# A gated attention and MLP mix on one core: where the keys are split, how the output products are tiled, and over how many keys the row maximum is taken

## The chip, the cores and the metric

The kernel runs on one core of one Trainium2 chip. The metric is device time in microseconds (us), the median of three runs. A profile of one execution stands beside it: when every instruction of the five engines began and ended (PE is TensorE, PEld its weight loads, DVE VectorE, ACT ScalarE, POOL GpSimd, SP SyncE, which here only issues transfers).

## What is computed

```python
# x: 2048 x 448, H = 16 heads of Dh = 28; one key and one value head for all (wk, wv: 448 x 28)
q = (x @ wq).reshape(S, H, Dh);  k = x @ wk;  v = x @ wv
p = softmax(q @ k.T * Dh ** -0.5)            # per head, 2048 x 2048
a = (p @ v).reshape(S, H * Dh) @ wo          # 2048 x 448
h  = gelu(layernorm(x) @ w1)                 # the four quarters of h are then shifted by +1, -1, +2, -2 rows
x1 = x + shifted(h) @ w2
b  = x1 + gelu(layernorm(x1) @ w3) @ w4      # w3: 448 x 1792
g  = sigmoid(x @ gate_w)
out = g * a + (1 - g) * b
```

## The kernel before

All values are fp32. Most products are taken in TensorE's faster fp32 format (fp32r) on split operands: an operand is cut into a high part that the format holds and a low part with the rest, and high x high, low x high and high x low are added up in one bank. The product of probabilities and values is plain fp32.

The program has three stages.

1. **Projections and the token mixing.** Queries, keys, values and the gate come out of one projection and are written to the DRAM buffer `qd`. `stage_w1` and `stage_w2` do the mixing for four blocks of 512 tokens. Towards the end the keys are read back, a quarter (512 keys) at a time, into one buffer `kf`: `load_k` (L332, eight transfers on SP's queue, four copies of the 28 rows on partitions 0, 32, 64 and 96), and `split_k` (L336, L337, both on POOL) cuts it into `kH` and `kL`. The buffer is filled with ones once, so that the rows behind the 28 hold ones. `load_k(0)` is issued before the first transfers of MLP weights (`load_w34`, L550 and L551) and the read of the normalised tokens (`xt_read`, L171, L173); the other three follow these.
2. **The MLP.** Four blocks `b` of 512 tokens, 14 slices `f` of 128 hidden columns each: `w3_part` (11 matmuls of 512 columns, L130 to L134), two gelus on ACT, and two slices later `w4_part` (12 matmuls of 448 columns, L641 to L643). The weights come in pairs of slices, pair `i` serving `f` = 2i and 2i+1. They are split on arrival: high parts and copies on ACT (L105, L107, L108, L557), low parts on DVE (L112, L113, L558), and POOL zeroes half of the last part of `w3h` (L106). The raw weights and the transposed tokens share two buffers (`big`), so pair 1 is loaded into the buffer that the tokens `xr` of block 0 leave, and pair 2 into that of pair 0.
3. **Attention.** The unit `u` (0 to 15) is 512 queries of four heads; inside it `kt` runs over 16 key tiles of 128. One step does 12 score matmuls (L828: three products for each of four heads, each head on its own 32 rows of the array, all four side by side, each head into a bank of its own), four exponentials of 128x512 on ACT (L832), and the value products of two steps ago (L808: four plain fp32 matmuls, each on its own 32 columns of the array, all into one bank). Seven banks rotate for scores and for the two extra jobs below. A column of ones in the values gives the row sums.

Extra jobs sit between a step's scores and its value products:
- `max_part` (L204, L205), four times for each coming unit: one matmul of 256 columns (four heads times `MK` = 64 keys) into a bank, and a maximum on DVE. The negated maximum is put in two spare rows of the next unit's queries (`max_end`, L224 to L232), so that the exponentials stay bounded. For units 1 to 15 the parts are made at `kt` 1, 3, 4 and 5 of the unit before (for unit 1 at 5, 7, 9 and 10); unit 0's are made in MLP block 2.
- `wo_job` (L769 to L771), four times for each unit gone by, at `kt` 8, 10, 12 and 14: three fp32r matmuls of 448 columns, 128 tokens by 448. Its left operand was normalised before: copy of the sums out of the bank (`o`, L736), transfers of the row sums out and back over DRAM (`rt`, `rd`, `rb`), the reciprocal, a multiplication on DVE (L754), and the split on POOL (L757, L758). Unit 0 has `w4_job` in its place.

Each engine runs its instructions in the order written. A last branch does all attention again with maxima over all keys if a row sum exceeds `LIMIT` = 1e12.

Of the kernel before, what the change touches and what calls it, by code (L numbers as in the profile page):

```python
# [9 lines left out]
F32 = mybir.dt.float32  # L10
F32R = mybir.dt.float32r
AF = mybir.ActivationFunctionType
# [20 lines left out]
MK = 64  # L33
# [3 lines left out]
def f32(ap):  # L37
    return ap.bitcast(F32)
# [3 lines left out]
def gated_mix_kernel(  # L42
# [157 lines left out]
    def max_part(u, t, tile_of):  # L200
        if t == 0:
            mx_of[u] = late.tile([P, 4, 4], F32, tag="mr", bufs=1, name=f"mr_{u}")
        ps = tile_of(f"m_{u}_{t}")[:, 0:4 * MK].rearrange("p (j k) -> p j k", j=4)
        nc.tensor.matmul(ps, qh_of[u][:, t * P:(t + 1) * P], khd, start=True, stop=True)  # L204
        nc.vector.reduce_max(mx_of[u][:, :, t], ps, axis=AX.X)  # L205
# [32 lines left out]
    with tc.tile_pool(name="s1b", bufs=1) as s1b, \  # L238
# [77 lines left out]
        kf = s1b.tile([P, 512], F32, name="kf")  # L316
        nc.gpsimd.memset(kf, 1.0)

# [9 lines left out]
        def load_k(b):  # L328
            for r in range(4):
                for g, n in ((0, 16), (1, DH - 16)):  # L330
                    at = 32 * r + 16 * g
                    nc.sync.dma_start(kf[at:at + n, :], rest(g, n, b))  # L332

        def split_k(b):
            cols = slice(512 * b, 512 * b + 512)
            nc.gpsimd.tensor_copy(kH[:, cols], kf)  # L336
            nc.gpsimd.tensor_tensor(kL[:, cols], kf, f32(kH)[:, cols], ALU.subtract)  # L337
# [191 lines left out]
        load_k(0)  # L529
# [77 lines left out]
    with tc.tile_pool(name="s2", bufs=1, reuse_waits="tile") as s2, \  # L607
# [5 lines left out]
        fills = [lambda t=t: max_part(0, t, max_tile if t % 2 else misc_tile) for t in range(4)]  # L613
        fills += [lambda: max_end(0)]
# [30 lines left out]
        for b in range(NB):  # L645
            acc = [ps2.tile([P, 512], F32, tag="acc", bufs=4, name=f"acc_{b}_{t}") for t in range(4)]
            gs = {}
            for f in range(NF):
# [24 lines left out]
                if b == 1 and f == 1:  # L673
# [4 lines left out]
                if b == 1 and f == 5:  # L678
                    q_split(0, qh0, ql0)
                if f >= 2:  # L680
                    for t in range(4):
                        w4_part(f - 2, t, gs[f - 2], acc)
                        if b > 1 and t % 2 == 0 and f < NF - 1:
                            fill()
# [15 lines left out]
    with tc.tile_pool(name="s3", bufs=1, reuse_waits="tile") as s3, \  # L700
            tc.tile_pool(name="ps3", bufs=1, space=PSUM, reuse_waits="tile") as ps3:
        woh = s3.tile([P, 4, D], F32R, name="woh")
        wol = s3.tile([P, 4, D], F32R, name="wol")

        banks = [mm_tile("bank_0"), mm_tile("bank_1"), misc_tile("bank_2")]
        banks += [ps3.tile([P, 512], F32, name=f"bank_{i}") for i in range(3, 7)]

# [26 lines left out]
        def sums_begin(u, pv):  # L734
            o = s3.tile([P, 512], F32, tag="o", bufs=2, name=f"o_{u}")
            nc.vector.tensor_copy(o, pv)  # L736
# [15 lines left out]
        def norm(u, o, rb):  # L752
            on = s3.tile([P, 512], F32, tag="onf", bufs=2, name=f"on_{u}")
            nc.vector.tensor_mul(on, o, rb)  # L754
            onh = s3.tile([P, 512], F32R, tag="onh", bufs=2, name=f"onh_{u}")
            onl = s3.tile([P, 512], F32R, tag="onl", bufs=2, name=f"onl_{u}")
            nc.gpsimd.tensor_copy(onh, on)  # L757
            nc.gpsimd.tensor_tensor(onl, on, f32(onh), ALU.subtract)  # L758
            on_of[u] = (onh, onl)
# [3 lines left out]
        def wo_job(u, t, end=None):  # L763
            b, g = divmod(u, NG)
            n = 4 * b + t
            tok = slice(t * P, (t + 1) * P)
            onh, onl = on_of[u]
            ps = bank(f"job_{n}")[:, 0:D]
            nc.tensor.matmul(ps, onh[:, tok], woh[:, g, :], start=True, stop=False)  # L769
            nc.tensor.matmul(ps, onh[:, tok], wol[:, g, :], start=False, stop=False)  # L770
            nc.tensor.matmul(ps, onl[:, tok], woh[:, g, :], start=False, stop=True)  # L771
            before = x1[:, n, :] if g == 0 else ot_of[n]
            if g == 0:
                ot_of[n] = s3.tile([P, D], F32, tag="ot", bufs=5, name=f"ot_{n}")
            if end:
                end(t, n, ps, before)
                return
            nc.vector.scalar_tensor_tensor(ot_of[n], ps, gg[:, n:n + 1], before, op0=ALU.mult, op1=ALU.add)  # L778
            if g == NG - 1:
                nc.sync.dma_start(out[0, n * P:(n + 1) * P, :], ot_of[n])  # L780

        woraw = s3.tile([P, 4, D], F32, name="woraw")
        nc.sync.dma_start(woraw, wo.rearrange("(g p) n -> p g n", p=P))
        nc.gpsimd.tensor_copy(woh, woraw)
        nc.gpsimd.tensor_tensor(wol, woraw, f32(woh), ALU.subtract)
# [15 lines left out]
        def pv_group(k):  # L801
            u, kt = divmod(k, NT)
            if kt == 0:
                pv_of[u] = max_tile(f"pv_{u}")
            pv = pv_of[u]
            ps = p_of.pop(k)
            for j in range(4):
                nc.tensor.matmul(pv[32 * j:32 * j + 32, :], vext[:, kt, :], ps[j],  # L808
                                 start=(kt == 0), stop=(kt == NT - 1), tile_position=(0, 32 * j))
            if kt == NT - 1 and u < NU - 1:  # L810
                sums.append(sums_begin(u, pv_of.pop(u)))

        WO_AT = (8, 10, 12, 14)
        M_AT = (1, 3, 4, 5)
        M_FIRST = (5, 7, 9, 10)
        LAG = 2

        for k in range(NU * NT + LAG):
            u, kt = divmod(k, NT)
            if k < NU * NT:  # L820
                if kt == 13 and u + 2 < NU:
                    q_begin(u + 2)
                    q_fetch(u + 3)
                bs = [bank(f"s_{4 * k + j}") for j in range(4)]
                for i in range(3):
                    for j in range(4):
                        for _, _, w, a in score(u, bs[j], j, slice(kt * P, (kt + 1) * P), i=i):
                            nc.tensor.matmul(bs[j], w, a, start=(i == 0), stop=(i == 2), tile_position=(32 * j, 0))  # L828
                p_of[k] = []
                for j in range(4):  # L830
                    p = s3.tile([P, 512], F32, tag="p", bufs=PB, name=f"p_{4 * k + j}")
                    nc.scalar.activation(p, bs[j], AF.Exp, scale=SCALE)  # L832
                    p_of[k].append(p)
                if kt == 3 and sums:
                    norms.append(recip(*sums.pop()))
                if kt == 6 and norms:
                    norm(*norms.pop())
                if kt in WO_AT:
                    t = WO_AT.index(kt)
                    if u:  # L840
                        wo_job(u - 1, t)
                    else:
                        w4_job(t)
                m_at = M_AT if u else M_FIRST
                if u + 1 < NU and kt in m_at:
                    t = m_at.index(kt)
                    max_part(u + 1, t, bank)
                    if t == 3:
                        max_end(u + 1)
            if k >= LAG:  # L850
                pv_group(k - LAG)
# [5 lines left out]
        onh = s3.tile([P, 512], F32R, tag="onh", bufs=2, name=f"onh_{u}")  # L857
        onl = s3.tile([P, 512], F32R, tag="onl", bufs=2, name=f"onl_{u}")
        on_of[u] = (onh, onl)
# [18 lines left out]
        def tail_back(t):  # L878
            nc.tensor.transpose(tq[t], on4[:, t], ident)
            nc.scalar.copy(onh[:, toks[t]], tq[t])  # L880

        def tail_low(t):
            nc.vector.tensor_sub(onl[:, toks[t]], tq[t], f32(onh)[:, toks[t]])
# [36 lines left out]
        tail_low(0)  # L920
        tail_on(3)
        tail_low(1)
# [6 lines left out]
        tail_low(2)  # L929
        tail_wo(0)  # L930
        tail_back(3)
        tail_low(3)
        tail_wo(1)
        tw = max_tile("worst_t")[0:1, 0:P]
# [10 lines left out]
        with tc.If(again > 0, label="redo"):  # L945
            for b in range(NB):
                for g in range(NG):
# [5 lines left out]
                    pv = max_tile(f"pv2_{u}")  # L953
# [9 lines left out]
                    norm(*recip(*sums_begin(u, pv), False))  # L963
                    for t in range(4):
                        wo_job(u, t)
# [51 lines left out]
```

## Time and profile before

| | us |
|---|---|
| median of 3 runs (lowest, highest) | 994.31 (994.22, 994.57) |
| the profiled execution, its time / its span | 995.8 / 994.0 |
| PE busy in the span | 970.8 (98%) |
| ACT busy | 651.9 (66%) |
| DVE busy | 287.1 (29%) |
| POOL busy | 107.5 (11%) |
| mean granted TensorE clock | 0.989 |

The rows in the prediction are of three kinds. A timeline row is: start, duration, engine, line, operation, output<-inputs, shape, number of instructions merged, and in brackets the idle time of that engine before it and what ended it. A row of a weight load (PEld) marks well where a group of matmuls begins. A row of the windows view is: the stretch, its length, busy time and instructions of PE, PEld, DVE, ACT and POOL, then the granted clock, the transfer engines' share and GB/s.

### The profile page before, as it was taken

The numbers are of one execution on the slowest core, as the hardware profiler recorded it, in microseconds if no ns is written. First come the engines' busy times: TensorE is split into PE (matmuls) and PEld (weight loads), VectorE is DVE, ScalarE is ACT, GpSimd is POOL, SyncE is SP. The second block draws the span as 40 slices with busy tenths as digits, with TensorE's granted clock in tenths as the row PEclk, the third lists the DMA queues.
The fourth block names the chain that finished last, engine by engine and source line by source line (L and its number), as shares of the span: only waits on it lengthen the run. The fifth ranks groups of instructions, "written<-read, shape, count | busy, mean of one in ns | idle before, by whom it ended". The sixth has DMA issues, their size and how long they took to land.

```text
span 994.0 us, 18445 instructions
## 1 busy us (share of the span) xinstructions
PE 970.8 (98%) x7251; PEld 562.5 (57%) x7251; DVE 287.1 (29%) x572; ACT 651.9 (66%) x1266; POOL 107.5 (11%) x134
## 2 busy tenths in 40 slices
PE   9999949999999999999999999999999999999997
PEld 6788838888888888843333333333333333333333
DVE  4663424631431431212222222212222221222112
ACT  5542315432232232299999999999998999999895
POOL 2241320100000520040000000000000000000000
PEclk9999969999999999999999999999999999999999
DMA  9703334130210300010000010000010000110001
GB/s 322 244 27 79 114 98 121 44 87 1 40 41 2 77 3 11 1 49 24 13 24 14 19 54 13 24 13 20 27 41 23 14 24 12 42 33 3 12 13 41
DMA packets 38750, 46.19 MB, mean 46 GB/s; under 512 B 8880, under 2 KB 27008, under 8 KB 38656
## 3 DMA queue, kind: packets, MB, share of 16 engines
q1 hardware_dynamic: 35632, 39.47, 13.4%
q10 hardware_dynamic: 3024, 5.47, 1.6%
q8 instruction: 59, 0.97, 0.4%
q14 instruction: 35, 0.29, 0.1%
HBM read 32.85 MB, written 11.67 MB: 45 GB/s over the span
## 4 chain that ended last, share of the span: by engine, by line
PE 94%; DMA 2%; SPq 1%; POOL 1%; DVE 0%; issue 0%; ACT 0%; POOLq 0%; DVEq 0%; ACTq 0%
PE pv L808 25%; PE bank L828 23%; PE acc L642 4%; PE acc L641 4%; PE acc L643 4%; PE g L131 4%; PE g L132 4%; PE g L130 4%; PE bank L769 2%; PE bank L204 2%; SPq L332 1%; PE g L133 1%; PE bank L771 1%; PE g L134 1%; PE bank L770 1%; PE h L130 1%
## 5 line engine op out<-in xcount | busy, mean ns | idle before, releaser
L832 ACT ACTIVATE p<-bank 128x512 f32<-128x512 f32 x1024 | 515.3, 640 | 47.9 <-PE bank L828 45.6
L808 PE MATMUL pv<-p,vext 128*32 128x512 f32 x2048 | 272.9, 604 | 0.0
L828 PEld LDWEIGHTS bank<-qh,kH 30*128 30x128 f32 x1024 | 51.7, 181 | 214.4 <-ACT p L832 212.9
L631 ACT ACTIVATE gh<-g 128x512 fp32r<-128x512 f32 x55 | 32.8, 597 | 183.6 <-PE g L134 183.6
L828 PE MATMUL bank<-qh,kH 30*128 30x512 f32 x1024 | 133.1, 494 | 0.4 <-ACT p L832 0.4
L828 PE MATMUL bank<-qh,kL 28*128 28x512 f32 x1024 | 105.7, 391 | 0.0
L828 PE MATMUL bank<-ql,kH 28*128 28x512 f32 x1024 | 105.6, 388 | 0.0
L633 DVE TENSOR_TENSOR gl<-gf,gh 128x512 fp32r<-128x512 f32 x55 | 38.5, 700 | 165.3 <-ACT gf L632 165.3
L808 PEld LDWEIGHTS pv<-p,vext 128*32 128x32 f32 x2048 | 40.6, 108 | 76.5 <-issue 62.8
L642 PE MATMUL acc<-w4l,gh 128*128 128x448 f32 x220 | 80.4, 366 | 0.0
L641 PE MATMUL acc<-w4h,gh 128*128 128x448 f32 x220 | 80.3, 365 | 0.0
L643 PE MATMUL acc<-w4h,gl 128*128 128x448 f32 x220 | 80.2, 365 | 0.0
L778 DVE SCALAR_TENSOR_TENSOR ot<-bank,gg,ot 128x448 f32<-128x448 f32 x44 | 30.1, 684 | 161.2 <-PE bank L771 122.6
L131 PE MATMUL g<-al,w3h 128*128 128x512 f32 x168 | 66.4, 395 | 0.0
L205 DVE TENSOR_REDUCE mr<-bank 128x4 f32<-128x256 f32 x60 | 25.6, 426 | 141.2 <-PE bank L204 141.2
L130 PE MATMUL g<-ah,w3h 128*128 128x512 f32 x168 | 66.3, 395 | 0.0
L132 PE MATMUL g<-ah,w3l 128*128 128x512 f32 x168 | 66.3, 395 | 0.0
L757 POOL CAST onh<-on 128x512 fp32r<-128x512 f32 x15 | 9.2, 611 | 493.0 <-DVE on L754 458.7
L828 PEld LDWEIGHTS bank<-ql,kH 28*128 28x128 f32 x1024 | 52.6, 185 | 9.1
L828 PEld LDWEIGHTS bank<-qh,kL 28*128 28x128 f32 x1024 | 51.9, 185 | 0.0
L641 PEld LDWEIGHTS acc<-w4h,gh 128*128 128x128 f32 x220 | 41.3, 188 | 4.7
L642 PEld LDWEIGHTS acc<-w4l,gh 128*128 128x128 f32 x220 | 41.3, 188 | 4.1
(196 smaller groups left out, 1096.2 us busy)
## 6 DMA issues: line engine op xcount, KB each, us to landing
qd<-qf ACTq DMA_DIRECT2D x16, 256.0 KB
qr<-qd SPq DMA_DIRECT2D x16, 256.0 KB
rb<-rd SPq DMA_DIRECT2D x15, 256.0 KB
x<-in_x_dram SPq DMA_DIRECT2D x4, 896.0 KB
xd<-xt SPq DMA_DIRECT2D x16, 224.0 KB
w34raw<-in_w_dram SPq DMA_DIRECT2D x7, 512.0 KB
out_dram<-ot SPq DMA_DIRECT2D x15, 224.0 KB
w34raw<-in_w_dram SPq DMA_DIRECT2D x7, 448.0 KB
```

The source lines that it names most:

```text
L130: nc.tensor.matmul(ps, wh[:, c, :], ah[:, c, :], start=(c == 0), stop=False)
L131: nc.tensor.matmul(ps, wh[:, c, :], al[:, c, :], start=False, stop=False)
L132: nc.tensor.matmul(ps, wl[:, c, :], ah[:, c, :], start=False, stop=False)
L631: nc.scalar.activation(gh, ps, AF.Gelu_apprx_tanh)
L633: nc.vector.tensor_sub(gl, gf, f32(gh))
L641: nc.tensor.matmul(ps, gh[:, tok], w4h[i][:, k, :], start=(f == 0), stop=False)
L642: nc.tensor.matmul(ps, gh[:, tok], w4l[i][:, k, :], start=False, stop=False)
L643: nc.tensor.matmul(ps, gl[:, tok], w4h[i][:, k, :], start=False, stop=(f == stop))
L778: nc.vector.scalar_tensor_tensor(ot_of[n], ps, gg[:, n:n + 1], before, op0=ALU.mult, op1=ALU.add)
L808: nc.tensor.matmul(pv[32 * j:32 * j + 32, :], vext[:, kt, :], ps[j], start=(kt == 0), stop=(kt == NT - 1), tile_position=(0, 32 * j))
L828: nc.tensor.matmul(bs[j], w, a, start=(i == 0), stop=(i == 2), tile_position=(32 * j, 0))
L832: nc.scalar.activation(p, bs[j], AF.Exp, scale=SCALE)
```

## The change

Four edits.

**Keys.** `load_k` and `split_k` go out of stage 1 and into MLP block 1: loads at `f` = 0, 2, 4, 6, splits at `f` = 1, 3, 5, 7. `kf` is now taken from the buffer `xn` (one buffer, used by the layernorm of a coming block at `f` = 10 and 11), and is filled with ones each time. The copies of the first keys into `khd` and the load and split of unit 0's queries go from block 1 to block 2, and unit 0's maxima from block 2 to block 3.

**Maxima.** `MK` is 32, and `max_all` makes all four parts at `kt` 5: four matmuls of 128 columns into one bank, one DVE maximum over 128x512.

**Output products.** `wo` and the normalised sums are no longer split. `wo_job` does four plain fp32 matmuls of 448 columns with 32 tokens each, on the four column tiles that the value products use. The reciprocal goes from `kt` 3 to 4 and the multiplication from 6 to 7.

**Bookkeeping.** Banks are taken from a list and given back after their last reader (`take`, `append`); the order of scores, extra jobs and value products in a step stays.

```diff
-MK = 64
+MK = 32
-    def max_part(u, t, tile_of):
-        ps = tile_of(f"m_{u}_{t}")[:, 0:4 * MK].rearrange("p (j k) -> p j k", j=4)
-        nc.tensor.matmul(ps, qh_of[u][:, t * P:(t + 1) * P], khd, start=True, stop=True)
-        nc.vector.reduce_max(mx_of[u][:, :, t], ps, axis=AX.X)
+    def max_all(u, ps):
+        for t in range(4):
+            nc.tensor.matmul(ps[:, t * P:(t + 1) * P], qh_of[u][:, t * P:(t + 1) * P], khd, start=True, stop=True)
+        nc.vector.reduce_max(mx_of[u].rearrange("p j t -> p t j"), ps.rearrange("p (t j k) -> p t j k", t=4, j=4), axis=AX.X)
...
-        load_k(0)
-            split_k(t) if t < 2 else None
-            load_k(t + 1) if t < 2 else None
         stage_w2(NB - 2, third)
-        split_k(2)
-        load_k(3)
-        split_k(3)
...
+                if b == 1 and f in (0, 2, 4, 6):
+                    load_k(f // 2, s2a.tile([P, 512], F32, tag="xn", bufs=1, name=f"kf_{f // 2}"))
+                if b == 1 and f in (1, 3, 5, 7):
+                    split_k(f // 2)
...
-            on = s3.tile([P, 512], F32, tag="onf", bufs=2, name=f"on_{u}")
-            nc.vector.tensor_mul(on, o, rb)
-            nc.gpsimd.tensor_copy(onh, on)
-            nc.gpsimd.tensor_tensor(onl, on, f32(onh), ALU.subtract)
+            nc.vector.tensor_mul(on_of[u], o, rb)
...
-            nc.tensor.matmul(ps, onh[:, tok], woh[:, g, :], start=True, stop=False)
-            nc.tensor.matmul(ps, onh[:, tok], wol[:, g, :], start=False, stop=False)
-            nc.tensor.matmul(ps, onl[:, tok], woh[:, g, :], start=False, stop=True)
+            for j in range(4):
+                tok = slice(t * P + 32 * j, t * P + 32 * j + 32)
+                nc.tensor.matmul(ps[32 * j:32 * j + 32, 0:D], on_of[u][:, tok], wof[:, g, :],
+                                 start=True, stop=True, tile_position=(0, 32 * j))
...
-        M_AT = (1, 3, 4, 5)
-        M_FIRST = (5, 7, 9, 10)
+        M_AT = 5
```

The order of the instructions on POOL at the end of stage 1, before: `hl` is the last work of the token mixing, then come the four key splits, then the zeroing of the MLP weights, pair 0 first.

```order
L415 MEMSET hl_915 112x4x2
L336 CAST kH<-kf 128x512
L337 TENSOR_TENSOR kL<-kf,kH 128x512
L336 CAST kH<-kf 128x512
L337 TENSOR_TENSOR kL<-kf,kH 128x512
L336 CAST kH<-kf 128x512
L337 TENSOR_TENSOR kL<-kf,kH 128x512
L336 CAST kH<-kf 128x512
L337 TENSOR_TENSOR kL<-kf,kH 128x512
L106 MEMSET w3h_1013 64x256
L106 MEMSET w3h_1166 64x256
```

The same place after:

```order
L414 CAST hl_686<-hl_913 112x4x2
L416 MEMSET hl_913 112x4x2
L106 MEMSET w3h_1003 64x256
L106 MEMSET w3h_1124 64x256
L106 MEMSET w3h_1169 64x256
```

The zeroing now follows the token mixing at once. SP's queue at the same place, after (`vT` is the read of the values):

```order
L322 DMA vT<-qd 16x1x512 x2
L550 DMA w34raw_1007<-in_w_dram 128x4x256
L551 DMA w34raw_1007<-in_w_dram 128x2x448
L171 DMA xr_1002<-xd_847 128x3x512
L173 DMA xr_1002<-xd_847 64x512 x2
L550 DMA w34raw_1128<-in_w_dram 128x4x256
L551 DMA w34raw_1128<-in_w_dram 128x2x448
```

Before, eight `kf` transfers stood between the first two rows and 24 between the last `xr` row and the load of weight pair 1.

PE in an attention step with an output product, before (the last scores, the product, the value products):

```order
L828 MATMUL bank_3210<-ql_3575,kH 128x512
L828 MATMUL bank_3211<-ql_3575,kH 128x512
L769 MATMUL bank_3212<-woh,onh_4306 128x448
L770 MATMUL bank_3212<-wol,onh_4306 128x448
L771 MATMUL bank_3212<-woh,onl_4307 128x448
L808 MATMUL pv_4181<-p_4296,vext 32x512
```

The same after:

```order
L799 MATMUL bank_3215<-ql_3568,kH 128x512
L799 MATMUL bank_3216<-ql_3568,kH 128x512
L763 MATMUL bank_3210<-wof,on_4315 32x448 x4
L822 MATMUL pv_4168<-p_6_0_4283,vext 32x512
L822 MATMUL pv_4168<-p_6_1_4285,vext 32x512
```

Three full-array matmuls between scores and values have become four on column tiles, next to others on the same tiles. PE in the step that makes the maxima, after:

```order
L799 MATMUL bank_3216<-ql_3568,kH 128x512
L799 MATMUL bank_3210<-ql_3568,kH 128x512
L203 MATMUL bank_3211<-khd,qh_4012 128x128 x4
L822 MATMUL pv_4168<-p_3_0_4185,vext 32x512
L822 MATMUL pv_4168<-p_3_1_4187,vext 32x512
```

Before, one row of that kind, 256 columns wide, stood at this place in four different steps.

More of the change, by code (lines that the diff above doesn't have):

```diff
@@ L799, in gated_mix_kernel, with scores, exps, late_exps @@
         p_of, pv_of, sums, norms = {}, {}, [], []
-        def pv_group(k):
-            u, kt = divmod(k, NT)
+        def scores(u, kt):
+            bs = [take() for j in range(4)]
+            for i in range(3):
+                for j in range(4):
+                    for _, _, w, a in score(u, bs[j], j, slice(kt * P, (kt + 1) * P), i=i):
+                        nc.tensor.matmul(bs[j], w, a, start=(i == 0), stop=(i == 2), tile_position=(32 * j, 0))
+            return bs
+        def exps(u, kt, bs):
+            ps = p_of[u, kt] = {}
+            for j in READ:
+                ps[j] = s3.tile([P, 512], F32, tag="p", bufs=PB, name=f"p_{u}_{kt}_{j}")
+                if j in DRAIN:
+                    nc.vector.tensor_copy(ps[j], bs[j])
+                else:
+                    nc.scalar.activation(ps[j], bs[j], AF.Exp, scale=SCALE)
+                banks.append(bs[j])
+        def late_exps(u, kt):
+            for j in DRAIN:
+                nc.scalar.activation(p_of[u, kt][j], p_of[u, kt][j], AF.Exp, scale=SCALE)
+        def values(u, kt):
             if kt == 0:
@@ L819, in gated_mix_kernel @@
             u, kt = divmod(k, NT)
[L820 to L849, printed above, removed]
@@ new lines, in gated_mix_kernel @@
+            if kt == 13 and u + 2 < NU:
+                q_begin(u + 2)
+                q_fetch(u + 3)
+            exps(u, kt, scores(u, kt))
+            late_exps(u, kt)
+            if kt == 4 and sums:
+                norms.append(recip(*sums.pop()))
+            if kt == 7 and norms:
+                norm(*norms.pop())
+            if kt == M_AT and u + 1 < NU:
+                ps = take()
+                max_all(u + 1, ps)
+                banks.append(ps)
+                max_end(u + 1)
@@ L850, in gated_mix_kernel @@
+            if kt in WO_AT:
+                if u:
+                    wo_add(*wo_job(u - 1, WO_AT.index(kt)))
+                else:
+                    w4_job(WO_AT.index(kt))
             if k >= LAG:
-                pv_group(k - LAG)
+                values(*divmod(k - LAG, NT))
+        for kt in range(NT - LAG, NT):
+            values(NU - 1, kt)
         assert not sums and not norms
@@ L879, in tail_back @@
             nc.tensor.transpose(tq[t], on4[:, t], ident)
[L880 to L883 removed]
+            nc.scalar.copy(on_of[u][:, toks[t]], tq[t])
         y = s3.tile([P, D], F32, name="y")
```

79 lines of the change are left out of this document (38 added, 41 removed).

## The prediction

> **What bounds the kernel now.** I read the windows view first, then the timeline of PE where a window is not full, then POOL, SP and ACT at that place, and last PE's weight loads in the attention loop.
>
> ```profile
> 100.00:125.00 25.00, 25.00 (x121) 21.53 (x120) 12.28 (x20) 9.63 (x16) 9.01 (x14) 1.00 0.34 109
> 125.00:150.00 25.00, 11.38 (x41) 9.08 (x40) 5.28 (x10) 3.46 (x6) 5.31 (x10) 0.66 0.31 98
> ...
> 500.00:600.00 100.00, 100.00 (x966) 38.26 (x966) 22.07 (x47) 91.96 (x184) 5.67 (x6) 1.00 0.09 27
> ```
>
> PE is full in the attention loop (500 to 600), and ACT close behind it with 92 of 100 us. So the loop pays for what PE issues, and gives back what is taken from PE only as long as ACT keeps up. The one hole lies at 125 to 150: PE busy 11.4 of 25 us, and the granted clock down to 0.66.
>
> ```profile
> 130.24 0.39 PE L132 MATMUL g<-ah,w3l 128*128 128x512 f32 x1
> 144.25 0.79 PE L133 MATMUL g<-ah,w3h 128*128 128x512 f32 x1 [13.62 <-POOL w3h L106]
> ...
> 149.53 0.61 PE L134 MATMUL g<-ah,w3l 128*128 128x512 f32 x1
> 149.96 0.41 PE L130 MATMUL g<-ah,w3h 128*128 128x512 f32 x1
> ...
> 152.50 0.36 PE L641 MATMUL acc<-w4h,gh 128*128 128x448 f32 x1
> ```
>
> ```profile
> 132.34 0.61 POOL L336 CAST kH<-kf 128x512 fp32r<-128x512 f32 x1 [8.05 <-DMA kf<-qd]
> 133.03 1.26 POOL L337 TENSOR_TENSOR kL<-kf,kH 128x512 fp32r<-128x512 f32 x1
> 141.88 0.61 POOL L336 CAST kH<-kf 128x512 fp32r<-128x512 f32 x1 [7.58 <-DMA kf<-qd]
> 142.57 1.26 POOL L337 TENSOR_TENSOR kL<-kf,kH 128x512 fp32r<-128x512 f32 x1
> 143.89 1.57 POOL L106 MEMSET w3h<- 64x256 f32 x6
> ```
>
> The first MLP slice stops in its tenth matmul, because POOL zeroes `w3h` only after the last key split, and each split waits some 8 us for its eight transfers. The hole has nothing to do with the weights themselves.
>
> **Edit 1, the keys.** With the splits gone from POOL the zeroing follows the token mixing, and L133 can start one matmul after L132. In the 11 matmuls from 149.96 to 152.50 one takes 2.54 / 11 = 0.23 us, so the start is 130.47 and the hole gives 144.25 - 130.47 = 13.8 us. The 13 matmuls from 144.25 to 149.96 took 5.71 us, 0.44 each, at the lowered clock; at 0.23 they take 3.0. That gives 2.7 us more. Together **16.5 us**.
>
> By the Trainium skill ("TensorE: Matmul & The Clock Gate", "What's actually happening") an idle array drops to half rate and about 3.4 us of busy time lifts that; at half rate 3.4 us lose 1.7 us, and the sum would be 1.0 us smaller. The row has 5.7 us at the low rate and decides.
>
> What is late next? The weights of pair 1, which slice 2 needs.
>
> ```profile
> 114.30 25.75 SPq L332 DMA_DIRECT2D kf<-qd  x24
> 140.16 0.61 SPq L550 DMA_DIRECT2D w34raw<-in_w_dram  x1
> 119.89 0.69 DVE L579 TENSOR_TENSOR ah<-xr,ah 64x512 fp32r<-64x512 f32 x1
> 125.03 1.07 DVE L558 TENSOR_TENSOR w4l<-w34raw,w4h 128x896 fp32r<-128x896 f32 x1
> 144.70 0.83 ACT L105 CAST w3h<-w34raw 128x768 fp32r<-128x768 f32 x1 [24.11 <-DMA w34raw<-in_w_dram]
> 146.63 0.41 DVE L113 TENSOR_TENSOR w3l<-w34raw,w3h 64x256 fp32r<-64x256 f32 x1
> ```
>
> SP issued that load only at 140.16, behind 24 key transfers (25.75 us of issue). Without them it needs its buffer, which the tokens leave at 119.89 + 0.69 = 120.6. From issue to the first cast took 4.5 us (140.16 to 144.70), from there to the last low part 2.3: ready at 127.5. Slice 2 starts after slices 0 and 1, at 130.47 + 0.46 + 2.54 = 133.5, so 6 us are to spare. Pair 2 follows in the buffer free at 126.1 and is needed two slices later still. No new wait.
>
> In block 1 the keys come back: four rounds of a fill, eight transfers and two POOL operations. A round took 141.88 - 132.34 = 9.5 us, with the fill an estimated 10 to 11, so four take about 42 us. POOL and SP have nothing else there until `f` = 10, where the layernorm wants `xn` back. Ten slices are about 50 us: one is the 2.54 above plus twelve `w4` matmuls of 448 columns, 0.2 us each at the same rate. PE waits for no key before attention. I take nothing for it; if DVE found `xn` still held at `f` = 10, the few us would be hidden by the two slices that remain. The moved query load and `khd` are five transfers with a block to spare.
>
> **Edit 2, the maxima.**
>
> ```profile
> 561.50 0.19 PEld L828 LDWEIGHTS bank<-qh,kH 30*128 30x128 f32 x4 [0.84 <-ACT p L832]
> ...
> 562.39 0.19 PEld L204 LDWEIGHTS bank<-khd,qh 128*128 128x128 f32 x1 [0.36 <-ACT p L832]
> 562.71 0.16 PEld L808 LDWEIGHTS pv<-p,vext 128*32 128x32 f32 x8
> 563.71 0.29 PEld L828 LDWEIGHTS bank<-qh,kH 30*128 30x128 f32 x4 [0.84 <-ACT p L832]
> ...
> 564.69 0.16 PEld L808 LDWEIGHTS pv<-p,vext 128*32 128x32 f32 x8 [0.35 <-DVE o L736]
> ```
>
> ```profile
> 110.47 0.56 PEld L342 LDWEIGHTS vp<-ident,vT 128*128 128x128 f32 x4
> 111.00 0.19 PEld L422 LDWEIGHTS hs<-w2h,hh 112*128 112x128 f32 x1
> ```
>
> A part costs PE 562.71 - 562.39 = 0.32 us, four in a unit 1.28. Much of that is the change of tiling around the single matmul: 256 columns stream in 0.23 x 256 / 512 = 0.115. Four matmuls together pay this once. No row shows 128 fp32r columns on the full array. Lower bound: pure streaming, 0.058 each. Upper bound: the plain fp32 rate of the value products (edit 3), 0.215. The nearest row is the four 128-column transposes of L342, 0.53 us, 0.13 each, and I take that. The group then costs (0.32 - 0.115) + 4 x 0.13 = 0.73 us (0.44 to 1.07), and a unit gains 0.55 (0.21 to 0.84). Over 15 units: **8.2 us** (3 to 12.6). The DVE maximum grows to one of 512 columns and has four steps until anyone asks.
>
> With no part at `kt` 1, a small wait goes too: the value products at 564.69 waited for the copy `o`, that step taking 564.69 - 563.71 = 0.98 for its scores where 0.89 is usual (561.50 to 562.39). 0.09 x 14: **1.2 us**.
>
> **Edit 3, the output products.**
>
> ```profile
> 574.24 0.19 PEld L828 LDWEIGHTS bank<-qh,kH 30*128 30x128 f32 x4 [0.84 <-ACT p L832]
> ...
> 575.14 0.16 PEld L808 LDWEIGHTS pv<-p,vext 128*32 128x32 f32 x8 [0.36 <-issue]
> 576.13 0.19 PEld L828 LDWEIGHTS bank<-qh,kH 30*128 30x128 f32 x4 [0.84 <-ACT p L832]
> ...
> 577.03 0.19 PEld L769 LDWEIGHTS bank<-woh,onh 128*128 128x128 f32 x1 [0.36 <-issue]
> ...
> 577.84 0.16 PEld L808 LDWEIGHTS pv<-p,vext 128*32 128x32 f32 x8 [0.31 <-issue]
> ...
> 978.77 0.13 PEld L808 LDWEIGHTS pv<-p,vext 128*32 128x32 f32 x4 [0.30 <-issue]
> ...
> 979.63 0.12 PEld L808 LDWEIGHTS pv<-p,vext 128*32 128x32 f32 x2 [0.30 <-ACT p L832]
> ```
>
> A plain step is 576.13 - 574.24 = 1.89 us: 0.90 of scores, 0.99 of values. The product adds 577.84 - 577.03 = 0.81. The new one has the form of the value products, which run 0.99 us between scores, but 979.63 - 978.77 = 0.86 where one such group follows another. The new product is followed by one, so the change of tiling is paid once for both, and it adds 0.86 x 448 / 512 = 0.75 us. Upper bound, with the change paid again: 0.99 x 448 / 512 = 0.87; no row shows such a group faster than 0.86, so 0.75 is the lower one too, and the nearer. I take it: 60 products x 0.06 = **3.6 us** (or -3.6 at the upper bound). So this edit is nearly even; four fp32 matmuls side by side cost what three fp32r ones did.
>
> It also takes POOL's split out of the chain before the product. That cover is good in most units (three maxima parts lengthen the way), but not in the last:
>
> ```profile
> 948.09 0.69 DVE L736 COPY o<-pv 128x512 f32<-128x512 f32 x1 [5.96 <-PE pv L808]
> 958.58 0.16 PEld L808 LDWEIGHTS pv<-p,vext 128*32 128x32 f32 x8 [0.37 <-issue]
> 959.36 0.69 DVE L754 TENSOR_TENSOR on<-o,rb 128x512 f32<-128x512 f32 x1 [8.36 <-DMA rb<-rd]
> ...
> 962.20 0.19 PEld L771 LDWEIGHTS bank<-woh,onl 128*128 128x128 f32 x1 [1.06 <-POOL onl L758]
> 962.60 0.16 PEld L808 LDWEIGHTS pv<-p,vext 128*32 128x32 f32 x8 [0.21 <-issue]
> ```
>
> That step took 4.02 us where 1.96 + 0.81 were due: **1.2 us**, gone when the product needs only L754 (done at 960.05, the scores at about 960.5). In the other units the way from `o` to the product is now as short as here plus one group of maxima, so the product finds its operand 0.4 us or more ahead.
>
> **What ACT takes back.**
>
> ```profile
> 943.32 19.71 ACT L832 ACTIVATE p<-bank 128x512 f32<-128x512 f32 x40 [0.58 <-PE bank L828]
> ```
>
> Forty exponentials in a row take 19.71 us, 1.97 a step, against PE's 1.89. Extra jobs gave ACT time to catch up; now `kt` 15 and 0 to 4 are six plain steps in a row. With three spare banks PE can, by estimate, run ahead for about four of them and follows ACT in the last two: 2 x 0.06 in 14 units, **-1.6 us**.
>
> The tail trades twelve fp32r matmuls (0.20 each) for four groups of 0.75 with changes of tiling around the transposes between them, an estimated **-0.6 us**, less if the dropped low parts were on its path.
>
> Sum: 16.5 + 8.2 + 1.2 + 3.6 + 1.2 - 1.6 - 0.6 = **28.5 us**. The profiled execution would go from 995.8 (span 994.0) to 967.3; the median of the runs lies 1.5 lower, so I predict 994.3 - 28.5 = **965.8 us**.
>
> **The rivals.**
>
> *The 128-column matmuls run at the plain fp32 rate.* Nothing in the trace excludes it. A group then costs 1.07 us and the time is 965.8 + 15 x 0.34 = 971 us. Twelve in 100.
>
> *The column tiles of the output product don't overlap fully.* Four value products in a group do, but those read four different moving tiles, and these read one and the same. At 0.87 us the time is 965.8 + 60 x 0.12 = 973 us. The Trainium skill ("TensorE: Matmul & The Clock Gate", "Measured speedup vs the span model") gives 3.07 for four tiles of rows, not 4; by that the product would take 0.98 us and the time would be 979.5. The back-to-back groups above speak against it. Eleven in 100.
>
> *The hole is filled by another wait.* If pair 1, or another release that the splits had covered, came as late as before, the 16.5 us of edit 1 would be lost: 982 us. Against it stands the slack of 6 us. Six in 100.
>
> *Slower: the four output products run one after another,* since they share the moving tile `wof`. One alone takes 0.75, four 3.0 us: 60 x (3.0 - 0.75) = 135 us, 1101 us. It decides against the change from 60 x d = 28.5, a product 0.48 us dearer, 1.23 us. All four value products also share a bank and do overlap. Three in 100. The repeat branch is no rival: worked out from the inputs drawn, the largest row sum is 2.6e9 with 64 keys and 3.0e10 with 32, under the limit of 1e12.
>
> **How the numbers follow.** The forecast itself has 68 in 100, with its own range 961 to 969 (the lower bound of the maxima, -4.4; no loss to ACT and tail, and half of a miss each way). The range for all reaches down to 959, where these favourable bounds add up, and up to 975, past the first two rivals; the last two, 9 in 100, lie outside. Faster by over 0.2% (about 2 us, what a measurement of this kernel can tell from no change): 0.96; within 0.2%: 0.01; slower: 0.03.
>
> **What would show it.** The window 125 to 150 would show PE full and a granted clock of 1.00. `max_all`'s group would measure 0.73 us between its first weight load and that of the values, the output product 0.75. PE's share should stay at 100 in the loop, and ACT's rise to about 94. The loop from first to last `o` should shorten by 0.8 us a unit. The prediction is wrong if PE has a new idle stretch in the first slices of the MLP, or waits for `on` at `kt` 8, or if the output products show no overlap.

## The result and the profile after

| | before | after |
|---|---|---|
| median (lowest to highest), us | 994.44 (994.22 to 996.14) | 965.61 (965.27 to 966.19) |
| ratio to before, 95% interval | 1 | 0.9703 (0.9691 to 0.9714) |
| the profiled execution, its time / its span | 995.8 / 994.0 | 965.27 / 963.5 |
| mean granted TensorE clock | 0.989 | 0.998 |

The change gives 28.8 us by the medians; 965.8 was forecast. The profiled execution of the kernel before was 1.4 us above its median and that of the changed kernel 0.3 below, so the two traces differ by 30.5. The same two windows as before, of the changed kernel:

```profile
125.00:150.00 25.00, 25.00 (x117) 21.58 (x116) 11.98 (x22) 11.91 (x23) 0.55 (x2) 1.00 0.49 158
500.00:600.00 100.00, 100.00 (x1048) 36.06 (x1048) 18.98 (x40) 94.01 (x190) 0.00 (x0) 1.00 0.09 27
```

The hole is gone, at a full clock. In the attention loop PE stays full, and ACT rises from 92 to 94 of 100 us. The timelines of PE in the first slices, then of POOL and SP:

```profile
127.34 0.40 PE L130 MATMUL g<-ah,w3h 128*128 128x512 f32 x1
...
129.19 0.39 PE L132 MATMUL g<-ah,w3l 128*128 128x512 f32 x1
129.41 0.39 PE L133 MATMUL g<-ah,w3h 128*128 128x512 f32 x1
...
134.85 0.36 PE L635 MATMUL acc<-w4h,gh 128*128 128x448 f32 x1
```

```profile
111.35 1.06 POOL L106 MEMSET w3h<- 64x256 f32 x4
...
196.18 0.61 POOL L337 CAST kH<-kf 128x512 fp32r<-128x512 f32 x1 [16.09 <-DMA kf<-qd]
...
227.54 0.61 POOL L337 CAST kH<-kf 128x512 fp32r<-128x512 f32 x1 [7.87 <-DMA kf<-qd]
188.20 37.23 SPq L332 DMA_DIRECT2D kf<-qd  x32
247.89 3.02 SPq L166 DMA_DIRECT2D xd<-xt  x4
```

L133 follows L132 by 0.22 us, where 13.62 us of waiting stood: POOL zeroed its part at 111.35, 16 us before the first slice. The 33 matmuls to the first `w4` product take 7.51 us, 0.23 each. The four key rounds in block 1 lie (227.54 - 196.18) / 3 = 10.45 us apart and end some 18 us before SP has its next work.

Three steps of the loop, by PE's weight loads. The first makes the maxima, the second copies the sums out (`o`), and the third, from another unit, has an output product:

```profile
548.03 0.27 PEld L799 LDWEIGHTS bank<-qh,kH 30*128 30x128 f32 x4 [0.84 <-ACT p L809]
...
549.01 0.52 PEld L203 LDWEIGHTS bank<-khd,qh 128*128 128x128 f32 x4 [0.36 <-issue]
549.61 0.16 PEld L822 LDWEIGHTS pv<-p,vext 128*32 128x32 f32 x8
```

```profile
542.32 0.19 PEld L799 LDWEIGHTS bank<-qh,kH 30*128 30x128 f32 x4 [0.84 <-ACT p L809]
...
543.22 0.16 PEld L822 LDWEIGHTS pv<-p,vext 128*32 128x32 f32 x8 [0.36 <-DVE o L826]
```

```profile
518.45 0.19 PEld L799 LDWEIGHTS bank<-qh,kH 30*128 30x128 f32 x4 [0.84 <-ACT p L809]
...
520.35 0.19 PEld L799 LDWEIGHTS bank<-qh,kH 30*128 30x128 f32 x4 [0.84 <-ACT p L809]
521.25 0.16 PEld L763 LDWEIGHTS bank<-wof,on 128*32 128x32 f32 x8 [0.36 <-ACT p L809]
...
522.99 0.19 PEld L799 LDWEIGHTS bank<-qh,kH 30*128 30x128 f32 x4 [0.84 <-ACT p L809]
```

The group takes 549.61 - 549.01 = 0.60 us. The step with a product takes 522.99 - 520.35 = 2.64, a plain one 1.90, so the product adds 0.74. From one unit to the next it is 34.05 us in the middle of the loop, 34.96 before: 0.91 less, where some 0.8 was forecast.

Where the span's 30.5 us came from, between marks that both traces have:

| stretch | before | after | difference | forecast |
|---|---|---|---|---|
| start to first `w3` matmul | 128.39 | 127.34 | -1.05 | 0 |
| from there to the first scores | 291.38 | 274.75 | -16.63 | -16.5 |
| from there to the last copy `o` | 528.32 | 514.96 | -13.36 | -11.4 |
| from there to the last values | 33.48 | 31.96 | -1.52 | -1.2 |
| the tail | 12.43 | 14.49 | +2.06 | +0.6 |

The first row is no effect of the change: the mark lies at 128.20, 127.56 and 127.52 in the three kernels below that hold one edit each.

### The profile page after: what moved, and what is told of

Read it like the earlier page. It is cut to its first block, busy times and chain, and to the rows that moved or that the text cites. A ratio compares the mean times of both kernels' runs of the same rounds, so it can differ in the third digit from the quotient of the medians.

```text
span 963.5 us, 18999 instructions
## 1 busy us (share of the span) xinstructions
PE 954.1 (99%) x7571; PEld 542.9 (56%) x7571; DVE 269.4 (28%) x520; ACT 647.1 (67%) x1266; POOL 75.0 (8%) x105
## 3 DMA queue, kind: packets, MB, share of 16 engines
q1 hardware_dynamic: 35632, 39.45, 13.8%
## 5 line engine op out<-in xcount | busy, mean ns | idle before, releaser
L822 PEld LDWEIGHTS pv<-p,vext 128*32 128x32 f32 x2048 | 46.8, 108 | 97.1 <-issue 89.9
L132 PE MATMUL g<-ah,w3l 128*128 128x512 f32 x168 | 65.6, 390 | 0.0
L763 PE MATMUL bank<-wof,on 128*32 128x448 f32 x512 | 61.2, 551 | 0.0
```

The lines of the kernel that those rows point to most:

```text
L132: nc.tensor.matmul(ps, wl[:, c, :], ah[:, c, :], start=False, stop=False)
L763: nc.tensor.matmul(ps[32 * j:32 * j + 32, 0:D], on_of[u][:, tok], wof[:, g, :], start=True, stop=True, tile_position=(0, 32 * j))
```

## The experiments

The kernel before had a median of 995.3 to 995.6 us beside these runs. Gains are given from the ratio, with its interval. The edits are shown shortened.

**One edit at a time.** Three kernels, each the kernel before with one edit: the keys in block 1; 32 keys and `max_all` at `kt` 5; plain fp32 products on column tiles.

```diff
# keys_only                                   # max_only                    # wo_only
-  load_k / split_k in stage 1                -MK = 64                      -3 matmuls onh/onl x woh/wol, split on POOL
+  load_k / split_k at b == 1, f = 0..7       +MK = 32, max_all at kt 5     +4 matmuls on x wof, tile_position=(0, 32 * j)
```

> The kernel before with the keys moved to MLP block 1, nothing else. Theory (POOL's order made the hole): the first MLP slice runs through, 16.5 us less than before, about 977.9 us, and the stretch from the first w3 matmul to the first scores shrinks from 291.4 us to about 275. Rival (the hole was covered by several things and edit 2 or 3 helped to close it): less than 12 us gained. Second rival (the 1.05 us by which the changed kernel was already ahead before the token mixing ended belongs to this edit, which takes a POOL fill out of the start): 976.8 us, and the lead is seen again before 108 us.

> The kernel before with the maxima over 32 keys in one group at kt 5, nothing else. Theory: a group costs 0.60 us in place of 4 x 0.32, and the small wait for the copy o goes: 15 x 0.68 + 1.2 less some 1.5 for ACT, about 984.5 us. The output product still waits for POOL's split, which is now covered by one group less: up to 1 us a unit may come back, which would give up to 995. Rival (128 columns run at the plain fp32 rate): a group of 1.07 us and about 992 us.

> The kernel before with the output product in plain fp32 on four column tiles, nothing else. Theory: 0.75 us in place of 0.82 a product, 60 times, 4.0 us less; 1.2 us less for the wait in the last unit; 1.3 to 2 us more in the tail: about 991 us. Rival (the product itself gains nothing, only the shorter way before it): 994 us, with the step of a product as long as before.

| kernel | median, us | ratio (interval) | gain, us |
|---|---|---|---|
| keys | 979.16 | 0.9834 (0.9815 to 0.9854) | 16.5 (14.5 to 18.4) |
| maxima | 985.21 | 0.9901 (0.9884 to 0.9918) | 9.9 (8.2 to 11.5) |
| products | 991.37 | 0.9960 (0.9946 to 0.9975) | 4.0 (2.5 to 5.4) |

The sum is 30.4, the whole change gives 29.5 (28.4 to 30.7) by its ratio: within their errors the edits add up. The keys alone fill the hole (the window of that kernel; below it the group of the kernel with the maxima alone):

```profile
125.00:150.00 25.00, 25.00 (x117) 21.64 (x116) 12.00 (x23) 12.33 (x22) 0.55 (x2) 1.00 0.50 157
```

```profile
565.58 0.52 PEld L203 LDWEIGHTS bank<-khd,qh 128*128 128x128 f32 x4 [0.36 <-issue]
566.17 0.16 PEld L806 LDWEIGHTS pv<-p,vext 128*32 128x32 f32 x8
```

The group's 0.59 us is the same with and without the other edits.

**The low clock behind the hole.** Was the forecast's 2.7 us really the price of an idle TensorE?

```diff
+        wps = misc_tile("hole_ps")         # in the first slice, between L132 and L133
+        for _ in range(120):
+            nc.tensor.matmul(wps[:, 0:256], warm[:, 0:P], warm, start=True, stop=True)
```

> The kernel before, with 120 small matmuls of zeros (128x256, 0.11 us each in the tail's rows, 13.4 us in all) in the hole of the first MLP slice, into a bank that nothing else uses there. The hole stays, only TensorE is busy in it. Theory (the 2.7 us of the forecast's first term are the low clock behind the hole, and it is TensorE's idling that lowers it): the 13 matmuls behind the hole take 3.0 us instead of 5.7, granted clock 1.00 in that window, the time 2 to 3 us under the kernel before. Rival (the matmuls behind the hole are slow for another reason, such as the transfers and splits that start there): they stay at 0.43 us each, time as before.

Measured 993.5 us, ratio 0.9984 (0.9973 to 0.9994), a gain of 1.6 us (0.6 to 2.7), where 2 to 3 were expected. Its PE timeline:

```profile
129.56 13.27 PE L136 MATMUL hole_ps<-warm 128*128 128x256 bf16 x120
143.37 0.50 PE L137 MATMUL g<-ah,w3h 128*128 128x512 f32 x1 [0.54 <-POOL w3h L106]
...
146.22 0.39 PE L138 MATMUL g<-ah,w3l 128*128 128x512 f32 x1
147.65 0.50 PE L130 MATMUL g<-ah,w3h 128*128 128x512 f32 x1 [1.03 <-ACT gf L637]
...
150.28 0.36 PE L646 MATMUL acc<-w4h,gh 128*128 128x448 f32 x1
```

The 13 matmuls take 146.22 + 0.23 - 143.37 = 3.1 us instead of 5.7: the clock was the cause, and keeping PE busy keeps it up (granted clock 1.00 from 128.4 to 150 us, where the kernel before shows 0.65 up to 143 and 0.50 from there). The time gains less than expected. Here half of the gain goes into a new wait of 1.2 us for a gelu on ACT, which in this kernel has the late weights of pair 1 to cast at the same time. From the first of these matmuls to the first `w4` product it is 6.91 us, against 152.50 - 144.25 = 8.25 before: 1.3 gained, not 2.6. With the keys moved, the weights come before the slices, and the whole 2.7 arrives.

**What a group of maxima costs.** Narrowing alone, grouping alone, pairs, and 16 keys:

```diff
# max_narrow (from before)     # max_grouped (from before)                # max_pairs (from before)       # keys16 (from after)
-MK = 64                       -M_AT = (1, 3, 4, 5)                       -M_AT = (1, 3, 4, 5)            -MK = 32
+MK = 32                       +all four at kt 5, 256 columns, two banks  +M_AT = (3, 5), two in a bank   +MK = 16
```

> The kernel before with the maxima over 32 keys instead of 64 (128 columns a matmul instead of 256), but still in four parts at four key tiles, each in a bank of its own. Theory (a part's 0.32 us is 0.2 us for the two changes of tiling and 0.12 for the matmul, of which narrowing takes 0.02 to 0.05): 60 parts give 1 to 3 us, 991 to 993 us. Rival (the columns set the price, half of them costs half): 0.16 us a part, 9.6 us, 985 us.

> The kernel before with the maxima still over 64 keys (256 columns a part), but all four parts together at kt 5 in two banks. Theory (what counts is the change of tiling paid once, and a 128-column matmul costs hardly less than a 256-column one, 0.10 against 0.115 us): a group costs 0.67 us, a gain within 1.5 us of that of the run with 32 keys. Rival (what counts is half the columns): a group costs what four parts cost, 1.28 us, and the time stays at 994.

> The kernel before with its four parts of 64 keys in two pairs at two key tiles, one bank a pair; the matmuls keep 256 columns. Theory (a fixed 0.2 us for each visit to the full array and 0.12 for each matmul, from 0.32 for one and 0.67 for four, and no second bank to wait for): a pair takes 0.44 us, a unit 0.88 instead of 1.28, 15 units give 6 us: 988 to 990. Rival (a step with a pair waits for banks or VectorE as the group of four did): the pair takes 0.44, the step behind it 0.2 us or more longer, 993 to 996.

> The changed kernel with the maxima over 16 keys (64 columns a matmul instead of 128). The group of four matmuls took 0.60 us with 128 columns, 0.67 with 256. Theory (with 128 columns the matmuls already wait for their 128x128 weights, whose loads lie 0.11 us apart): the group stays at 0.57 to 0.60 us, and the time within 1 us of the changed kernel's 965.6. Rival (the columns set it): a matmul of 128 columns took some 0.10 us, one of 64 takes 0.05, the group 0.40, and 15 units give 3 us: 962.6.

| kernel | columns | matmuls in a visit | visit, us | median, us | ratio (interval) |
|---|---|---|---|---|---|
| before | 256 | 1 | 0.32 | 995.4 | 1 |
| max_pairs | 256 | 2 | 0.43 | 988.76 | 0.9935 (0.9919 to 0.9952) |
| max_grouped | 256 | 4 | 0.67 | 992.06 | 0.9964 (0.9951 to 0.9977) |
| max_narrow | 128 | 1 | 0.26 | 993.20 | 0.9988 (0.9974 to 1.0001) |
| after | 128 | 4 | 0.60 | 965.61 | 0.9703 (0.9691 to 0.9714) |
| keys16 | 64 | 4 | 0.57 | 965.37 | 0.9702 (0.9688 to 0.9717) |

The times of after and keys16 hold the other edits too. Weight loads of keys16, of max_narrow, and of max_pairs:

```profile
549.32 0.52 PEld L203 LDWEIGHTS bank<-khd,qh 128*128 128x128 f32 x4 [0.36 <-issue]
549.89 0.16 PEld L822 LDWEIGHTS pv<-p,vext 128*32 128x32 f32 x8
```

```profile
560.54 0.19 PEld L204 LDWEIGHTS bank<-khd,qh 128*128 128x128 f32 x1 [0.36 <-ACT p L832]
560.80 0.16 PEld L808 LDWEIGHTS pv<-p,vext 128*32 128x32 f32 x8
```

```profile
563.49 0.30 PEld L211 LDWEIGHTS bank<-khd,qh 128*128 128x128 f32 x2 [0.36 <-ACT p L840]
563.92 0.16 PEld L816 LDWEIGHTS pv<-p,vext 128*32 128x32 f32 x8
```

A further matmul in a visit costs (0.67 - 0.32) / 3 = 0.117 us at 256 columns and (0.60 - 0.26) / 3 = 0.113 at 128, and halving the columns again to 64 saves 0.03 in a group of four. So a matmul of 128 columns or fewer is not paid by its columns: four weight loads of 128 columns are merged to 0.52 us where one is 0.19, (0.52 - 0.19) / 3 = 0.11 apart, and that is the price. The Trainium skill ("TensorE: Matmul & The Clock Gate", "LDWEIGHTS (loading the stationary operand)") prices a weight load by its own columns, P / 1.2 ns, which by estimate is 107 ns for 128; the distance of 0.11 us between the loads here agrees. The rest of a visit, 0.15 to 0.20, is fixed. Of the 0.68 us that a unit gained (4 x 0.32 - 0.60), grouping gives most, whichever comes first: narrowing first gives 4 x (0.32 - 0.26) = 0.24 and grouping then 4 x 0.26 - 0.60 = 0.44; grouping first gives 4 x 0.32 - 0.67 = 0.61 and narrowing then 0.07.

Narrowing alone should give 15 x 0.24 = 3.6 us by its visits; measured are 1.2 (-0.1 to 2.6), which is not clear of no change. Its trace shows where a part goes: the scores behind the part at `kt` 1 take 1.05 us (561.79 to 562.84) where they took 0.98, since the bank that they want still waits for an exponential.

**Why the group of four parts in two banks gained so little.** Its visits save 15 x (1.28 - 0.67) = 9.2 us, its time only 3.6 (2.3 to 4.9): neither the theory (within 1.5 us of the run with 32 keys, which gains 9.9) nor the rival (nothing) came true. The pairs save less in visits (15 x 0.42 = 6.3) and gain 6.5 (4.8 to 8.1). The weight loads of max_grouped:

```profile
569.22 0.54 PEld L210 LDWEIGHTS bank<-khd,qh 128*128 128x128 f32 x4 [0.37 <-issue]
569.89 0.16 PEld L816 LDWEIGHTS pv<-p,vext 128*32 128x32 f32 x8
570.88 0.19 PEld L834 LDWEIGHTS bank<-qh,kH 30*128 30x128 f32 x3 [0.84 <-ACT p L838]
571.27 0.18 PEld L834 LDWEIGHTS bank<-qh,kH 30*128 30x128 f32 x1 [0.19 <-ACT p L838]
...
572.16 0.16 PEld L816 LDWEIGHTS pv<-p,vext 128*32 128x32 f32 x8 [0.37 <-issue]
```

The next scores find three banks and wait for the fourth: they take 572.16 - 570.88 = 1.28 us instead of 0.90, and 15 x 0.38 = 5.7 us. To tell the second bank from the 256 columns, the changed kernel got a second bank too:

```diff
-                ps = take()
-                max_all(u + 1, ps)
+                pair = [take() for i in range(2)]      # two parts of 128 columns in each
+                max_all(u + 1, pair)
```

> The changed kernel with its four maxima matmuls of 128 columns in two banks of two, each with a maximum of its own on VectorE, instead of in one bank. Theory (what ate two thirds of the gain when the four parts of 64 keys were put together is the second bank: the next scores then wait for one exponential more): the group takes 0.60 us as in the changed kernel, the step behind it 2.2 to 2.3 us instead of 1.90, 15 units give 5 to 6 us: 970 to 972. Rival (it was the 256 columns, or the longer maxima of VectorE, that made that step long): 965 to 967.

```profile
551.35 0.52 PEld L203 LDWEIGHTS bank<-khd,qh 128*128 128x128 f32 x4 [0.36 <-issue]
551.94 0.16 PEld L824 LDWEIGHTS pv<-p,vext 128*32 128x32 f32 x8
552.94 0.19 PEld L801 LDWEIGHTS bank<-qh,kH 30*128 30x128 f32 x3 [0.84 <-ACT p L811]
553.40 0.18 PEld L801 LDWEIGHTS bank<-qh,kH 30*128 30x128 f32 x1 [0.28 <-ACT p L811]
...
554.27 0.16 PEld L824 LDWEIGHTS pv<-p,vext 128*32 128x32 f32 x8 [0.35 <-issue]
```

Measured 973.07 us (972.40 to 973.41), 7.5 above the changed kernel and 1 above the upper end that was expected. The group is 0.59, as with one bank; the scores behind it take 1.33 us, 0.43 more than usual, 6.5 us in 15 units. Half of the remaining 1 us lies ahead of the loop (first scores at 402.61 instead of 402.09); the other half I did not follow. It is the bank: the columns are those of the changed kernel, and the late load waits for an exponential (ACT). In the group, narrowing to 32 keys is worth 0.07 us a unit in TensorE time, and 0.4 by letting the four parts fit into one bank.

**Does the product gain by standing next to the values?**

```diff
             for i in range(3):                 # in scores(), the three score passes
+                if i == 2 and u and kt in WO_AT:
+                    jobs.append(wo_job(u - 1, WO_AT.index(kt)))
```

> The changed kernel, with each of the loop's 60 output products put between the second and the third score pass of its key tile instead of between the scores and the values; nothing is left out. Theory (the products gained because they now share the 128x32 column tiles with the values that follow them, and the array's change of tiling is paid once, not twice): in the kernel before, a product on the full array took 0.82 us, of which three matmuls of 448 columns at one column a cycle are 0.56, so 0.26 went to two changes of tiling; between score passes the product has two changes of its own, so it costs 0.95 to 1.0 us instead of 0.75, 60 times: 977 to 981 us. Rival (a product costs its 0.75 us wherever it stands, and the gain was that of the arithmetic alone): 964 to 967 us, third pass 0.75 us late.

Measured 1002.84 us (1002.44 to 1002.97), 37 above the changed kernel and slower than the kernel before (ratio 1.0076, 1.0061 to 1.0092). The PE timeline:

```profile
541.74 0.51 PE L801 MATMUL bank<-qh,kH 30*128 30x512 f32 x4
542.08 0.41 PE L801 MATMUL bank<-qh,kL 28*128 28x512 f32 x4
542.42 0.96 PE L763 MATMUL bank<-wof,on 128*32 128x448 f32 x8
543.31 0.51 PE L801 MATMUL bank<-ql,kH 28*128 28x512 f32 x4
543.74 1.07 PE L824 MATMUL pv<-p,vext 128*32 128x512 f32 x8
544.74 0.78 PE L801 MATMUL bank<-qh,kH 30*128 30x512 f32 x4
...
545.91 1.06 PE L824 MATMUL pv<-p,vext 128*32 128x512 f32 x8
```

The theory is right in kind and short in size. Scores with the product in them take 543.74 - 541.74 = 2.00 us, plain ones 0.90 as in the changed kernel: the product adds 1.10 where 0.95 to 1.0 was expected, so two more changes of tiling cost 0.36, not 0.2 to 0.25. And the scores of the next step take 545.91 - 544.74 = 1.17 us, 0.27 more: the exponentials began 1.1 us later, and their banks come free later. Together 1.10 + 0.27 - 0.74 = 0.63 us, 60 times, is 38. The Trainium skill ("TensorEngine Tiling (Array Packing)", "Key Properties") says that a change of tiling mode drains the engine. The rows here put 0.18 us on each change; that a drain is what takes it they do not show.

**The tail.** The last four products as before, three fp32r matmuls on the full array; the loop as changed:

```diff
             ps = take()
+            if end:                            # behind the loop: onh, onl, woh, wol on the full array
+                for i, (a, w) in enumerate(((onh, woh), (onh, wol), (onl, woh))):
+                    nc.tensor.matmul(ps[:, 0:D], a[:, tok], w[:, g, :], start=(i == 0), stop=(i == 2))
+            else:                              # in the loop: four column tiles, as changed
```

> The changed kernel, but the last four products, behind the loop, are done as before: split fp32r, three matmuls on the full array, with the low part of the normalized values by VectorE. The loop is as in the changed kernel. Theory (the tail lost 1.0 us on TensorE because there the product stands between transposes of the full array and has no values next to it): from the first of the last products to TensorE's end 2.9 us as in the kernel before instead of 3.95, the time 0.8 to 1.5 us under the changed kernel's 965.6. Rival (the tail's loss of 2.06 us is the landing of the last writes, which varies from run to run): the products are shorter, the end is where it was, 965.6 within 0.4.

The PE timeline of the changed kernel's tail, of the kernel before's, and of this one's, first and last products:

```profile
951.69 0.96 PE L763 MATMUL bank<-wof,on 128*32 128x448 f32 x8
952.58 0.33 PE L885 MATMUL bank<-ident,on 128*128 128x128 f32 x1
952.84 0.96 PE L763 MATMUL bank<-wof,on 128*32 128x448 f32 x8
...
953.93 1.71 PE L763 MATMUL bank<-wof,on 128*32 128x448 f32 x16
```

```profile
984.08 0.45 PE L769 MATMUL bank<-woh,onh 128*128 128x448 f32 x1
...
986.62 0.37 PE L771 MATMUL bank<-woh,onl 128*128 128x448 f32 x1
```

```profile
952.32 0.45 PE L769 MATMUL bank<-woh,onh 128*128 128x448 f32 x1
...
954.86 0.37 PE L769 MATMUL bank<-woh,onl 128*128 128x448 f32 x1
```

From the first product to PE's end it is 3.95 us in the changed kernel, 2.91 before, and 2.91 here. The tail as a whole is 12.59 us again, against 14.49 and 12.43, so what had seemed to be later landing of the last writes (0.8 us of the 2.06) went away with it. That part has a row too:

```profile
956.49 1.51 SPq L898 DMA_DIRECT2D out_dram<-ot  x1
```

SP takes 1.51 us to issue the last write in the changed kernel, and 0.33 in the kernel before and in this one. All five kernels whose last products stand on column tiles show 1.17 to 1.67 there, all eight others 0.33. Why the products should do this no run shows.

The time is 964.43 us (963.85 to 964.76), 1.2 under the changed kernel, as the theory said. The five runs lie below all four of the changed kernel's (965.27 to 966.19) and all four of keys16 taken beside them (964.87 to 966.46), but 1.2 us is 0.12%, and the intervals of the ratios (0.9678 to 0.9705, 0.9691 to 0.9714) overlap. It is the fastest version run.

## Why the prediction was right

- **Keys: 16.5 forecast, 16.6 by the trace, 16.5 (14.5 to 18.4) alone.** Hole and clock are both as read; with PE kept busy the clock alone gives 2.6 at that place. No new wait: pair 1's last low part ended at 127.0 (forecast 127.5), and a key round took 10.45 us (10 to 11). The rival with another wait in the hole is out.
- **Maxima: 8.2 forecast, 10.2 by the group's row.** This term was mis-sized. The step that failed took the transposes of L342, 0.13 us each, as the nearest row and charged four of them on top of the fixed part. A further matmul costs 0.11, and the fixed part falls from 0.20 to 0.15 with the columns: 0.60 us, not 0.73. The rival with the plain fp32 rate (1.07 us) is out. What I did not see is that one bank decides: the same group in two would have given back 6.5 to 7.5 us.
- **The wait for `o`: 1.2 forecast.** The time is there, but the wait was misread. In the kernel before, the copy was done at 563.85 + 0.69 = 564.54, and the scores alone, started at 563.71, would have held PE until 564.61. What is long in that step is the scores' own row of weight loads, 0.29 us instead of 0.19: the fourth starts 0.1 us late and waits for an exponential, which has to give back a bank. After the change the step with the copy takes its usual 0.90 (542.32 to 543.22) with `o` named as before.
- **ACT: -1.6 forecast.** The two steps before the group take 1.92 and 1.97 us where 1.90 is plain, about 0.1 a unit, as forecast. The row at 548.03 (0.27 us, scores of 0.98) shows the same wait for a bank. So the two terms are one wait, which moved from behind the part at `kt` 1 to the steps before the group. Together 14 x 0.08 gained and 15 x 0.10 lost come to -0.4, the same as 1.2 - 1.6; for the first of the two that is luck.
- **Products: 3.6 forecast, 3.3 by the traces.** Over all 60 the product adds 0.80 us before and 0.75 after, 60 x 0.055. The 0.75 is as read from the back-to-back value products; the 0.81 of the old one was read from a single step. The edit alone gains 4.0 (2.5 to 5.4), where its three terms were 3.6 + 1.2 - 0.6 = 4.2. The four tiles overlap fully though they share the moving operand: the rivals with partial overlap and with none are out. The reason given, one change of tiling for product and values together, is borne out by moving the product away, where two more changes cost 0.36 us. I had called the edit nearly even; moving the product costs 37 us, some 22 of them for changes of tiling and 16 for the banks that come free later.
- **The last unit: 1.2 forecast, 1.5 measured.** The product there starts right behind its scores. Four products at 0.055 are 0.2 of it.
- **The tail: -0.6 forecast, -2.06 measured.** The second mis-sized term, by a factor of three. Its -0.6 is 4 x 0.75 - 12 x 0.20, which leaves nothing for the changes of tiling it names: 3.95 us instead of 2.91 on PE. Another 0.8 us is the later end of the writes.

The maxima's 2.0 too little and the tail's 1.5 too much nearly cancel, so the 0.2 us between forecast and result are better than the terms deserve. The loop's terms as measured (10.2 for the maxima, 3.1 for the 56 products before the last `o`, -0.4 for the waits, together 12.9) come to 0.5 less than its 13.36.

## What to carry to other kernels

Price an extra job in a full TensorE loop by three things: the change of tiling on each side (0.18 us here), weight loads where the matmuls are short (0.11 us for 128 columns), and the banks it holds while the next scores want theirs (0.4 us for one bank more). A wait that a row names is a cost only if the step is longer than one without it: `o` was named in steps of 0.98 us and of 0.90. Put a job next to work of the same tiling, and make it small enough for one bank before making it shorter. When one engine stops for a queue entry of another engine that waits for transfers, moving those entries is worth the stall plus the low clock behind it.

## What the runs showed of the hardware

- Four plain fp32 matmuls on four column tiles that read one moving operand overlap as fully as four with an operand each: 0.74 us for 448 columns, four in all, against 0.86 x 448 / 512 = 0.75.
- A further fp32r matmul with new weights on the full array costs 0.11 to 0.12 us at 256 and at 128 columns; 64 columns bring next to nothing (0.57 us for four instead of 0.60).
- 120 small matmuls of zeros in a 13.8 us stall kept the granted clock at 1.00; without them 13 matmuls ran at 0.44 us instead of 0.23, at a granted clock of 0.50.
